# Attention followed by a squared-relu MLP on one core: exp sums ahead of relus, MLP blocks of 192 and 256 tokens, exp sums wholly on VectorE, three transposes one unit later

## Chip, core and metric

The kernel runs on one core of one Trainium2 chip. The metric is the device time of one execution in microseconds (us). Most executions of one kernel agree within 0.3%. A ratio in this document is the mean time of one kernel's fast runs over the mean of the other's fast runs of the same rounds, so it is not quite the ratio of the medians that are quoted beside it. The profiled span is 1.7 to 1.9 us shorter than the time, as it starts with the first instruction and ends with the last.

## The reference, cut to what matters

```python
# q, k, v: 8 batches x 12 heads x 448 tokens x 64; w_in: 768 x 2048; w_out: 2048 x 768
scores = scale * q @ k.T
e = exp(scores - m)
attn = e / (sum(e) + exp(-m) + 1e-9)      # a softmax with one more term in the sum
x = attn @ v                              # rearranged to 3584 tokens x 768
h = x @ w_in
out = relu(h)**2 @ w_out
```

## The kernel before

TensorE does the matmuls, ScalarE (ACT) the exp, VectorE (DVE) the additions, relus and squares. A **unit** is a pair of heads of one batch. Batch 0 is cut in two halves of 192 and 256 tokens, so units 0 to 11 are batch 0, and units 12 to 17 batch 1. The other six batches run in a loop of 18 **cycles** of two units each, three cycles to a batch. MLP work is woven in between: `ins` is a list of tiles of the first matmul (768 to 2048) of the batch before, `outs` one of the second. `drain` takes single matmul pairs from `ins` up to a time, `run` whole tiles, `rows(n)` takes `n` pairs from `outs`.

The MLP tile, with its eviction on VectorE, and the row sums, whose reciprocal takes a Ln and an Exp on ScalarE:

```python
def tile_in(t0, n, f0, per):
    hp = mp_tile()                       # one PSUM bank, one of four in turn
    for j in range(per):                 # per groups of 128 d_ff columns in one bank
        for dc in range(DCH):            # 6 chunks of d_model
            product(...)                 # two matmuls on the two column halves, n columns
    # relu: VectorE, but the tile with t0 == 0 and f0 == 8 on ScalarE
    nc.vector.tensor_mul(gs[...], r, r)

def row_sums(us, sums):
    zp = mp_tile()
    # ... matmuls with ones: the sums over keys (L243)
    nc.scalar.activation(out=rcp, in_=zp, func=AF.Ln, bias=one_b)      # L246
    nc.scalar.activation(out=rcp, in_=rcp, func=AF.Exp, scale=-1.0)    # L247
```

The exp sums of a unit are three VectorE additions of its four key chunks (`add_chunks`, steps 0, 1 and 2, the last adds the two halves). One loop cycle, cut:

```python
scores(ua, ea, 0); rows(11); scores(ua, ea, 1); add_chunks(ua, ..., 0); rows(11)
scores(ub, eb, 0); add_chunks(ua, ..., 1); add_chunks(ua, ..., 2); rows(10)
scores(ub, eb, 1); add_chunks(ub, ..., 0)
# ... values and normalise of the two units of the cycle before
n = (3, 7, 6)[pr // 2]                   # MLP tiles of this cycle
run(ins, n - 3)
add_chunks(ub, eb, sb, hb, 1)
add_chunks(ub, eb, sb, hb, 2)
run(ins, 2)
for at in (i, i + 1):
    rcps[at] = row_sums([units[at]], (ess.pop(at)[0:1],))
run(ins, 1)
```

In the traces VectorE runs its instructions in the order of the program: in the cycle at 117 us three relus start at 112.88, 114.02 and 115.15 us, then the two sums at 116.12 and 116.77, then the fourth relu at 117.31, as the code above has them. So a sum that stands behind a relu in VectorE's queue waits for the MLP tile of that relu, and a relu behind a sum waits for the exps.

The softmax here doesn't subtract the row's maximum and nothing guards it: scores larger than these inputs give would overflow.

## Time and profile before

| | before |
|---|---|
| time, median of three | 427.88 us |
| profiled span | 426.0 us |
| units 12 to 17, apart | 5.3 us |
| loop cycles of a batch (3, 7, 6 tiles) | 15.38, 17.31, 16.18 us |

### The profile page before, as it was taken

To read this page: it belongs to the slowest core of one execution; us is meant where nothing else is said; L and a number is where in the kernel's file an instruction comes from. 1 tells how busy PE (TensorE), PEld (TensorE's weight loads), DVE (VectorE), ACT (ScalarE), POOL (GpSimd) and SP (SyncE) were. 2 spreads that over 40 slices of the span, in tenths; PEclk is the share of its full clock that TensorE was granted. 3 is DMA by queue.
4 is the path that set the end of the run, shared out by engine and by line. 5 is a ranking of instruction groups with operands and counts; after the bars stand their busy time and mean duration, and the time that the engine had idled before them with its cause. 6 is when DMAs were issued, how large, how long until landed. Compare 5 with 4: busy or idle time off the path is not lost.

```text
span 426.0 us, 10689 instructions
## 1 busy us (share of the span) xinstructions
PE 410.8 (96%) x4715; PEld 271.7 (64%) x4715; DVE 278.1 (65%) x537; ACT 236.5 (56%) x328; POOL 36.5 (9%) x58
## 2 busy tenths in 40 slices
PE   8879999899999999999999999999999999999996
PEld 3566666565676675775776765775766766655563
DVE  4766778767775868668675769658676678377000
ACT  3989888664485384583575564773755754200211
POOL 7423310020000200002000300001000000000000
PEclk9999999999999999999999999999999999999999
DMA  9999999789109940199507871098001101100222
GB/s 201 197 198 196 191 199 197 141 124 201 39 2 218 177 110 2 48 183 180 134 2 167 157 143 38 38 194 144 38 2 38 38 2 38 39 37 0 75 74 75
DMA packets 75679, 45.58 MB, mean 107 GB/s; under 512 B 42544, under 2 KB 71856, under 8 KB 75312
## 3 DMA queue, kind: packets, MB, share of 16 engines
q0 software_dynamic: 28848, 22.16, 34.2%
q1 hardware_dynamic: 46064, 22.05, 22.0%
q8 instruction: 37, 0.61, 0.6%
q10 hardware_dynamic: 720, 0.69, 0.5%
q14 instruction: 10, 0.08, 0.1%
HBM read 45.69 MB, written 17.93 MB: 149 GB/s over the span
## 4 chain that ended last, share of the span: by engine, by line
PE 75%; DVE 10%; ACT 6%; DMA 5%; issue 2%; POOL 1%; ACTq 0%; POOLq 0%
PE mp L279 18%; PE mp L329 15%; PE mp L281 11%; PE xp L279 6%; PE sp L194 5%; PE mp L229 5%; PE xp L329 5%; DVE rt L299 4%; DMA kn<-in_k_dram 4%; ACT et L162 3%; PE xp L281 3%; PE xp L229 3%; PE sp L182 3%; DVE es L209 2%; DMA vn<-in_v_dram 2%; DVE half L207 2%
## 5 line engine op out<-in xcount | busy, mean ns | idle before, releaser
L162 ACT ACTIVATE et<-sp 112x896 f16<-112x896 f32 (+2 forms) x192 | 165.2, 913 | 25.8 <-PE sp L182 14.6
L279 PE MATMUL mp<-xt,win 128*64 128x448 f16 (+2 forms) x1260 | 113.2, 324 | 4.1 <-DVE xt L258 1.9
L279 PEld LDWEIGHTS <-win 128*64 128x64 f16 x1536 | 84.8, 110 | 50.4 <-issue 9.1
L329 PE MATMUL mp<-wout,gs 64*128 64x384 f16 x864 | 103.1, 322 | 0.0
L329 PEld LDWEIGHTS <-gs 64*128 64x128 f16 x1152 | 70.8, 94 | 18.5
L299 DVE TENSOR_SCALAR rt<-mp 128x448 f16<-128x448 f32 (+2 forms) x104 | 62.8, 604 | 23.2 <-PE mp L279 19.7
L246 ACT ACTIVATE rcp<-mp,one_b 128x448 f32<-128x448 f32 (+2 forms) x38 | 23.9, 630 | 67.5 <-PE mp L243 67.5
L301 DVE TENSOR_TENSOR gs<-rt 128x448 f16<-128x448 f16 (+2 forms) x132 | 50.8, 385 | 4.9 <-ACT rt L297 0.4
L329 PE MATMUL xp<-wout,gs 64*128 64x384 f16 x288 | 52.6, 322 | 0.0
L207 DVE TENSOR_TENSOR es<-et 112x896 f16<-112x896 f16 x42 | 26.0, 620 | 22.8 <-ACT et L162 22.8
L194 PE MATMUL sp<-qk 64*112 64x224 f16 x480 | 36.7, 261 | 1.2 <-ACT et L162 1.2
L194 PEld LDWEIGHTS <-qk 64*112 64x112 f16 x480 | 29.5, 128 | 9.2 <-issue 7.3
L338 ACT ACTIVATE ot<-mp 128x384 f32<-128x384 f32 x29 | 14.3, 493 | 35.0 <-PE mp L281 26.6
L281 PEld LDWEIGHTS <-gs 128*128 128x128 f16 x240 | 23.4, 98 | 15.8 <-issue 0.4
L229 PEld LDWEIGHTS <-vn 112*64 112x64 f16 x432 | 22.7, 109 | 15.2 <-issue 4.6
L281 PE MATMUL mp<-wout,gs 128*128 128x384 f16 x192 | 31.9, 326 | 0.0
L279 PE MATMUL xp<-xt,win 128*64 128x448 f16 x276 | 30.0, 353 | 0.5 <-DVE rt L299 0.5
L247 ACT ACTIVATE rcp<-rcp 128x448 f32<-128x448 f32 (+2 forms) x48 | 27.7, 577 | 1.5
L340 DVE SCALAR_TENSOR_TENSOR ot<-mp,ot 128x384 f32<-128x384 f32 x27 | 15.1, 558 | 19.4 <-ACT ot L338 18.1
L207 DVE TENSOR_TENSOR half<-et 112x896 f16<-112x896 f16 x42 | 25.9, 617 | 0.0
L299 DVE TENSOR_SCALAR rt<-xp 128x448 f16<-128x448 f32 x27 | 16.8, 623 | 13.0 <-PE xp L281 8.3
L182 PE MATMUL sp<-qk 64*112 64x448 f16 (+2 forms) x192 | 24.0, 321 | 1.2 <-ACT et L162 0.5
(62 smaller groups left out, 316.6 us busy)
## 6 DMA issues: line engine op xcount, KB each, us to landing
vn<-in_v_dram POOLq DMA_DIRECT2D x7, 672.0 KB, 8.5
out_dram<-ot SPq DMA_DIRECT2D x9, 384.0 KB, 2.3
win<-in_moe_w_in_dram POOLq DMA_DIRECT2D x8, 384.0 KB, 14.0
wout<-in_moe_w_out_dram POOLq DMA_DIRECT2D x4, 768.0 KB, 13.6
stage_q<-in_q_dram POOLq DMA_DIRECT2D x4, 676.0 KB, 11.2
stage_k<-in_k_dram POOLq DMA_DIRECT2D x4, 676.0 KB, 14.7
out_dram<-ot SPq DMA_DIRECT2D x8, 288.0 KB, 2.6
out_dram<-ot SPq DMA_DIRECT2D x10, 192.0 KB, 2.7
```

The lines of the kernel that those rows point to most:

```text
L162: nc.scalar.activation(out=out_, in_=in_, func=AF.Exp, scale=scale)
L182: nc.tensor.matmul(sp[:, h, o:o + n], qk[r, 1, x + P * kk:x + P * kk + P], qk[r, 0, x + q0:x + q0 + n], start=True, stop=True)
L194: nc.tensor.matmul(sp[:, odd, h * (S // 2):(h + 1) * (S // 2)], qk[r, which, kx:kx + 2 * P - 1:2], qk[r, 0, x:x + S // 2], start=True, sto ...
L207: nc.vector.tensor_add((es, half[:, 0:2 * S])[step], e[:, 2 * step], e[:, 2 * step + 1])
L229: nc.tensor.matmul(xp[64 * h:64 * h + 64, o:o + n], vns[b][:, 2 * pr + h, kk, :], of_head(chunk(et, u, kk // 2, kk), u, h), start=(kk == 0 ...
L246: nc.scalar.activation(out=rcp[:, 0:m], in_=zp[:, 0:m], func=AF.Ln, bias=one_b)
L247: nc.scalar.activation(out=rcp[:, 0:m], in_=rcp[:, 0:m], func=AF.Exp, scale=-1.0)
L279: nc.tensor.matmul(out_[x:x + 64], lhsT[:, x:x + 64], rhs, start=start, stop=stop)
L281: nc.tensor.matmul(out_, lhsT, rhs, start=start, stop=stop)
L299: nc.vector.tensor_scalar(out=rt[:, 0:m], in0=hp[:, 0:m], scalar1=0.0, scalar2=None, op0=ALU.max)
L301: nc.vector.tensor_mul(gs[:, f0:f0 + per, t0 % RING:t0 % RING + n], r, r)
L329: nc.tensor.matmul(o[:, 0:w], g[x:x + 64], wout[x:x + 64, fb, n0:n0 + w], start=(fb == 0), stop=(fb == NFFB - 1))
```

## The change

It has four parts: in 12 of 18 cycles the second pair's sums stand ahead of all but one relu; batch 0's MLP blocks have 192 and 256 tokens, two d_ff groups to a bank; units 12 to 16 add their exp sums wholly on VectorE (a third addition), so TensorE does one pair of row-sum matmuls instead of two; the transposes of batch 1's first three pairs come one unit later (units 9, 10 and 11; the others were at 12 to 14 already), and so do the first loads of batch 2. The intent is fewer waits of TensorE for VectorE, fewer and wider evictions, and no wait for batch 1's loads.

```diff
-        if t0 == 0 and f0 == 8:
-            nc.scalar.activation(out=rt[:, 0:m], in_=hp[:, 0:m], func=AF.Relu)
-        else:
-            nc.vector.tensor_scalar(out=rt[:, 0:m], in0=hp[:, 0:m], ..., op0=ALU.max)
+        nc.vector.tensor_scalar(out=rt[:, 0:m], in0=hp[:, 0:m], ..., op0=ALU.max)
 ...
-        per = max(1, 512 // n) if n < 256 else 1
+        per = max(1, 512 // n)
 ...
-        transpose_at[NPAIR + 2 + pr + pr // 3] = (1, pr)
+        transpose_at[NPAIR + 3 + pr] = (1, pr)
 ...
-            queue(0, 128)
-            share[0] = left() / NPAIR
+            queue(0, FIRST)                      # FIRST = 192
+            share[0] = left() / (NPAIR + 2)
 ...
-        if i == NPAIR + 4:                       # issues loads of batch 2
+        if i == NPAIR + 5:
 ...
-        drain(share[0] * 0.45)
+        drain(left() * 0.5 if first else share[0] * 0.45)
 ...
-            rcp = row_sums(done, (ess.pop(i - 1),))
+            rcp = row_sums(done, (ess.pop(i - 1)[0:1],))
 ...
-        for step in range(2):
+        for step in range(3):
             add_chunks(u, et, es, half, step)
-            drain(share[0] * 0.2)
+            drain(share[0] * (0.15, 0.1, 0.15)[step])
 ...
-            queue(128, S - 128)
+            queue(FIRST, S - FIRST)
 ...
-        run(ins, n - 3)
+        if pr:
+            run(ins)
+            n -= 1
         add_chunks(ub, eb, sb, hb, 1)
         add_chunks(ub, eb, sb, hb, 2)
-        run(ins, 2)
+        run(ins, n - 1)
         for at in (i, i + 1):
             rcps[at] = row_sums([units[at]], (ess.pop(at)[0:1],))
-        run(ins, 1)
+        run(ins)
```

More of the change, by code (lines that the diff above doesn't have):

```diff
@@ L295, in tile_in @@
         rt = r_pool.tile([128, 512], FP16, name="rt")
-        if t0 == 0 and f0 == 8:
-            nc.scalar.activation(out=rt[:, 0:m], in_=hp[:, 0:m], func=AF.Relu)
-        else:
-            nc.vector.tensor_scalar(out=rt[:, 0:m], in0=hp[:, 0:m], scalar1=0.0, scalar2=None, op0=ALU.max)
+        nc.vector.tensor_scalar(out=rt[:, 0:m], in0=hp[:, 0:m], scalar1=0.0, scalar2=None, op0=ALU.max)
         r = rt[:, 0:m].rearrange("p (j n) -> p j n", j=per)
@@ L514 @@
             done = [prev]
-            rcp = row_sums(done, (ess.pop(i - 1),))
+            rcp = row_sums(done, (ess.pop(i - 1)[0:1],))
             values(prev, ets.pop(i - 1), xp)
         drain(share[0] * 0.15)
-        for step in range(2):
+        for step in range(3):
             add_chunks(u, et, es, half, step)
-            drain(share[0] * 0.2)
-        if i == 3 * NPAIR - 1:
-            add_chunks(u, et, es, half, 2)
-            ess[i] = (es,)
-            if ins and ins[0][0] < ins[0][1]:
-                run(ins)
+            drain(share[0] * (0.15, 0.1, 0.15)[step])
+        if i == 3 * NPAIR - 1 and ins and ins[0][0] < ins[0][1]:
+            run(ins)
         normalise(done, xp, rcp)
         if first:
-            queue(128, S - 128)
+            queue(FIRST, S - FIRST)
             share[0] = left() / (NPAIR + 0.3)
@@ L564 @@
             if at not in rcps:
-                rcps[at] = row_sums([units[at]], (ess.pop(at),))
+                rcps[at] = row_sums([units[at]], (ess.pop(at)[0:1],))
             xp = mp_tile()
@@ L583 @@
         n = (3, 7, 6)[pr // 2]
-        run(ins, n - 3)
+        if pr:
+            run(ins)
+            n -= 1
         add_chunks(ub, eb, sb, hb, 1)
         add_chunks(ub, eb, sb, hb, 2)
-        run(ins, 2)
+        run(ins, n - 1)
         for at in (i, i + 1):
             rcps[at] = row_sums([units[at]], (ess.pop(at)[0:1],))
-        run(ins, 1)
+        run(ins)
         if pr == NPAIR - 2:
```

## The prediction

> **What bounds the kernel now.** I read the page first: the busy line, then the chain that ended last.
>
> ```profile
> PE 410.8 (96%) x4715; PEld 271.7 (64%) x4715; DVE 278.1 (65%) x537; ACT 236.5 (56%) x328; POOL 36.5 (9%) x58
> PE 75%; DVE 10%; ACT 6%; DMA 5%; issue 2%; POOL 1%; ACTq 0%; POOLq 0%
> ```
>
> TensorE has work in flight for 411 of 426 us, so there is little idle time to recover; but a tenth of the chain is DVE. The timeline splits the run in three: 0 to 69.7 us is attention of batches 0 and 1 with the first MLP blocks mixed in (18 units; unit 7 starts near 21.7), 69.7 to 363.7 is a loop of 18 cycles (6 batches of three), and after that TensorE streams matmuls to the end. The change leaves the last part alone. Next I read the waits in total:
>
> ```profile
> PEld L243 <- DVE es L209: 4.5, 13, 0.8
> PE mp L279 <- DVE rt L299: 1.5, 10, 0.2
> PE sp L194 <- ACT et L162: 1.2, 5, 0.3
> ```
>
> In a loop cycle the row-sum matmuls (L243) wait for the exp sums (L209), and the MLP tile behind them waits for a relu (L299) to free its PSUM bank. That is the target of the reordering. The third line is as important: five cycles wait for ScalarE instead. Here is the cycle around 117 us, which has the DVE wait, and then the one around 132 us, a first cycle of a batch, where the sums are already ahead of all relus (timelines; start, duration, engine, line):
>
> ```profile
> 117.21 0.36 PE L243 MATMUL mp<-es,ones 112*64 112x448 f16 x2
> 117.61 0.64 ACT L246 ACTIVATE rcp<-mp,one_b 128x448 f32<-128x448 f32 x1 [5.85 <-PE mp L243]
> 117.98 1.33 PE L279 MATMUL mp<-xt,win 128*64 128x448 f16 x12 [0.15 <-DVE rt L299]
> 119.89 1.71 ACT L162 ACTIVATE et<-sp 112x896 f16<-112x896 f32 x2
> 121.46 0.59 PE L194 MATMUL sp<-qk 64*112 64x224 f16 x8
> 123.63 0.59 PE L194 MATMUL sp<-qk 64*112 64x224 f16 x8
> ```
>
> ```profile
> 132.59 0.36 PE L243 MATMUL mp<-es,ones 112*64 112x448 f16 x2
> 132.97 1.30 PE L279 MATMUL mp<-xt,win 128*64 128x448 f16 x12
> 132.99 0.64 ACT L246 ACTIVATE rcp<-mp,one_b 128x448 f32<-128x448 f32 x1 [1.97 <-PE mp L243]
> 137.03 0.40 PE L194 MATMUL sp<-qk 64*112 64x224 f16 x4 [0.25 <-ACT et L162]
> 139.00 0.60 PE L194 MATMUL sp<-qk 64*112 64x224 f16 x8
> ```
>
> From the first row sum to the second pair's scores the first takes 123.63 - 117.21 = 6.42 us, the second 139.00 - 132.59 = 6.41 us. In the first, the MLP tile starts 0.77 us after the row sum; in the second 0.38 us. The second lost its 0.39 us lead at 137.03, waiting for an exp.
>
> In the first part the timeline shows these stalls:
>
> ```profile
> 26.98 0.39 PE L153 MATMUL mp<-ident,kn 112*64 112x112 f16 x8 [0.99 <-DMA kn<-in_k_dram]
> 28.21 1.02 ACT L162 ACTIVATE et<-sp 112x1024 f16<-112x1024 f32 x1 [1.68 <-PE sp L182]
> 39.06 0.39 PE L153 MATMUL mp<-ident,qn 112*64 112x112 f16 x8
> 44.68 0.60 PE L279 MATMUL mp<-xt,win 128*64 128x320 f16 x6 [0.99 <-DVE xt L258]
> 66.00:71.00 5.00, 5.00 (x62) 3.30 (x58) 4.09 (x10) 4.25 (x7) 0.00 (x0) 1.00 1.28 240
> ```
>
> Batch 1's first transpose waits for its k load; ScalarE idles 1.68 us behind it. At 44.68 an MLP tile of the second block waits for normalised activations. In the last row (a 5 us window; busy PE, PEld, DVE, ACT) TensorE has no gap, and DVE and ScalarE are over 80% busy.
>
> **What the Trainium skill says.** "TensorE: Matmul & The Clock Gate", section "Back-to-back issue gap", says that the spacing of weight-load and matmul pairs is set by both operations, so narrow matmuls cost more than their columns. The trace agrees: at 28.67 us 18 loads and their 128-wide matmuls take 0.60 us, 67 ns a pair on the two column halves, where 128/2.4 is 53; 22 matmuls of 320 columns take 1.50 us of the chain at 52.37, 136 ns a pair, where the columns alone are 133. "VectorE: DVE Perf Modes", section "The TRN2 errata — SBUF-src ops pay a fixed extra latency per instruction", gives a cost of a constant plus elements. The trace agrees in form: relus of 512 and 320 columns take 685 and 486 ns, so 1.04 ns a column and 154 ns fixed. "TensorEngine Tiling (Array Packing)", section "PSUM Bottleneck", advises evacuating several tiles of one bank together, which is what two d_ff groups to a bank do. "Perfetto Trace Analysis", section "Optimization Strategy", says the most contended engine may differ by regime; the windows above agree.
>
> **The change part by part.**
>
> *Sums ahead of relus, 12 of 18 cycles* (a batch's first cycle is the same in both). In the cycle of 117 us VectorE now does relu 1 (112.88), both sums, then relus 2 to 4. With the trace's spacings (relu plus multiply 0.97 us, the two sums 1.19) relu 4 ends near 117.60 in place of 117.93, and the second row sum no longer waits for 117.40. The tile can start at about 117.60: 0.35 us earlier; in the seven-tile cycle 0.40. Taken alone, 12 x 0.38 = 4.5 us. But ScalarE cannot start before the row sum at 117.21, which does not move. Its queue (two Ln, two exp for reciprocals, two exps of scores) runs from 117.61 to 121.60 without a gap, and TensorE needs that last exp's PSUM buffer for the second half of the scores at 121.46. It would arrive near 121.08 and wait. The cycle of 132 us shows this end state, only 0.01 us shorter. So I count 0.01 to 0.02 us a cycle: 0.2 us in all.
>
> *Blocks of 192 and 256 in place of 128 and 320.* Both have 96 column pairs a block (16 groups x 6). Before: 96 x 67 ns + 96 x 133 = 19.2 us of TensorE. After: 96 x 80 + 96 x 107 = 17.9 us, 1.3 less. Evictions on VectorE: before 3 x 685 + 4 x 426 + 16 x (486 + 325) = 16.7 us, plus a relu of 0.59 on ScalarE; after, on the fitted line, 8 x (552 + 359) + 8 x (685 + 426) = 16.2. The one on ScalarE joins them.
>
> *Third add in units 12 to 16.* Five adds of 0.62 us more on VectorE (+3.1), five second row-sum pairs of 0.19 us less on TensorE (-0.95).
>
> *Transposes one unit later.* The 1.0 us stall at 26.98 goes, and unit 8's second exp can follow its predecessor at 26.53 in place of 28.21. TensorE would reach unit 12's scores near 37.3 in place of 38.2. There the load of pairs 3 to 5 lands: issued at 23.84, 14.6 us to landing, so 38.4; the transposes now at 39.06 can begin near 38.5. The drain after them is now half of what is left, 16 pairs of 80 ns (1.28 us) where there were 8 narrow ones (0.54). Unit 12's second scores come out at about 40.1, as now: this lead is gone, except that more MLP work is behind.
>
> *Units 13 to 17.* With pairs of the first block left over, unit 13 need not wait at 44.68 for the normalisation; but ScalarE is then the limit (the exps of unit 12, Ln, exp, exps of unit 13), and only about 0.5 us is left of that 1. Each later unit now takes 5.3 us. It loses one row-sum pair (0.19) and does 19 pairs of 107 ns in place of 18 of 133 (0.37): 5.3 - 0.56 = 4.74 with transposes. ScalarE needs 4 exps in 3.45, Ln 0.65 and exp 0.58: 4.67. So ScalarE caps it almost at once, and VectorE's spacings sum to about 4.4. I allow 0.4 us a unit, not 0.56: 4 x 0.4 = 1.6, plus 0.5 for the start, and 0.2 at unit 15, whose exp wait shrinks. Unit 17 pays back 7 pairs, 0.75 us, for finishing the second block, and the first loop cycle then lacks the six pairs at 78.97 (0.8): a wash, with about 0.7 gained since the next tile starts in the slot where the leftover now waits for a bank.
>
> Sum: 0.5 + 1.6 + 0.2 + 0.7 + 0.2 = 3.2, less 0.3 for queueing between three engines over 90% busy: 2.9 us.
>
> **The rivals.** First, the DVE wait in the loop is pure loss and 4.5 us come back too: 420 us. The totals of waits speak for it, the 6.41 against 6.42 us against it. Second, the third add makes VectorE the bound of units 13 to 17: it is strictly in order, so a relu behind a sum waits for the exps, and row sums then wait for L209. The 4.09 busy in 5 us speaks for it, the wider relus against; all the gain there would go: about 426.5. Third, a load takes the place of the stall removed: loads into batch 1 and the second-batch issues, now a unit later. The 38.4 us landing speaks for it at unit 12, and I counted it; for later ones the queue has work from earlier issues until about 52 us, so they should stay hidden. A full reload stall would cost 1 us: 426.
>
> **Range and chances.** 427.88 - 2.9 = 425.0 us. Low: a third of the loop's waits come back too and units shrink by the full 0.56, 422.8. High: VectorE queueing eats most of the first part, 427.0. Two per cent is 8.6 us, more than all removed waits and work (4.5 + 1.3 + 0.95 + 1.0) if a part of it is hidden as argued: faster 0.02, within 0.97, slower 0.01.
>
> **What would show it.** Right: L243's wait for L209 nearly gone, L194's wait for L162 present in 15 or more cycles with about 4 us in total, and loop cycles of the same length to 0.05 us; the first loop scores (69.71 now) near 67.5; a DMA wait in unit 12's transposes; the 0.99 us at 44.68 gone. Wrong: loop cycles shorter by 0.3 us (rival one), L243 waiting for L209 between 45 and 70 us (rival two), or units of 5.3 us as now.

## More of the kernel before

For units 13 to 17, here are two windows of the profile of the kernel before. The columns are the window, its length, then the busy time and number of instructions of TensorE, its weight loads, VectorE, ScalarE and GpSimd, then the granted TensorE clock, the DMA share and GB/s.

```profile
50.00:55.00 5.00, 5.00 (x60) 3.43 (x58) 4.09 (x10) 4.24 (x6) 4.97 (x7) 1.00 1.29 175
60.00:65.00 5.00, 5.00 (x68) 3.44 (x64) 4.10 (x11) 4.24 (x7) 0.00 (x0) 1.00 1.35 202
```

TensorE has no gap, VectorE is at 82% and ScalarE at 85%. Three engines are close to full, so work that is moved from one to another needs room where it arrives.

To compare traces I use **marks**: the start of the first values matmul (L229) in a unit or a cycle. The code up to unit 6 is the same in all kernels here, but the first mark lies anywhere between 10.7 and 12.0 us in the profiles, so a comparison of marks counts from unit 6.

## The result

The changed kernel takes 425.26 us (median of four, 425.04 to 426.18), against 427.89 us before: a ratio of 0.9945, with a 95% interval of 0.9927 to 0.9962. The 2.6 us lie well outside the spread of both, but under 2%. The profiled span went from 426.0 to 423.3 us. The head and the chain of the changed kernel's page:

```profile
PE 408.8 (97%) x4705; PEld 273.3 (65%) x4705; DVE 277.7 (66%) x535; ACT 235.0 (56%) x327; POOL 36.7 (9%) x58
PE 70%; ACT 17%; DVE 9%; issue 3%; ACTq 0%
```

ScalarE's share of the chain has gone from 6% to 17%, and DMA is no longer on it. The waits of the changed kernel within its loop say why (who waited for whom: us in total, times, longest):

```profile
PE sp L194 <- ACT et L162: 3.4, 15, 0.3
PEld L243 <- DVE es L209: 1.0, 1, 1.0
```

The row sums' wait for the exp sums is down from 13 times to one, and the scores wait for an exp 15 times instead of five. This is the cycle that was shown at 117 us in the prediction, now at 115 us (timeline of the changed kernel):

```profile
114.80 0.55 PE L243 MATMUL mp<-es,ones 112*64 112x448 f16 x4
115.20 0.63 ACT L246 ACTIVATE rcp<-mp,one_b 128x448 f32<-128x448 f32 x1 [5.85 <-DVE rt L296]
115.23 1.33 PE L279 MATMUL xp<-xt,win 128*64 128x448 f16 x12
119.24 0.40 PE L194 MATMUL sp<-qk 64*112 64x224 f16 x4 [0.18 <-ACT et L162]
121.22 0.60 PE L194 MATMUL sp<-qk 64*112 64x224 f16 x8
```

The MLP tile starts 0.43 us after the row sum where it was 0.77. But from the row sum to the second pair's scores it is 121.22 - 114.80 = 6.42 us, as before. The lead is handed over at 119.24.

Where the time went, by marks (values of each unit or cycle), in us from unit 6's mark:

| from unit 6 to | before | after | gained in this step |
|---|---|---|---|
| unit 12 | 20.55 | 20.26 | 0.29 |
| unit 13 | 25.93 | 25.35 | 0.29 |
| unit 17 | 47.14 | 45.05 | 1.51 |
| first loop cycle | 56.59 | 54.98 | -0.48 |
| second loop cycle | 71.71 | 69.00 | 1.10 |
| values after the last cycle | 343.26 | 340.19 | 0.36 |

The sum is 3.07 us; 0.30 of it is lost again because this profile's unit 6 lies at 20.50 in place of 20.20. All loop cycles from the second on have the old lengths to 0.01 us: 18.09, 16.18, 15.37, 17.31. What the loop's new order gains is 0.35 us after the last cycle, where no scores follow that could wait for an exp.

In units 13 to 17 the change did its work, and the profile shows what sets the pace now. First three windows of the changed kernel, then single rows of its timeline:

```profile
50.00:55.00 5.00, 4.69 (x60) 3.02 (x57) 3.30 (x7) 4.74 (x8) 4.39 (x6) 1.00 1.38 192
55.00:60.00 5.00, 5.00 (x74) 3.46 (x73) 4.93 (x10) 4.45 (x7) 0.00 (x0) 1.00 1.33 201
60.00:65.00 5.00, 4.95 (x74) 3.46 (x73) 3.73 (x8) 4.74 (x7) 0.00 (x0) 1.00 1.36 204
```

```profile
38.41 0.39 PE L153 MATMUL mp<-ident,qn 112*64 112x112 f16 x8
45.31 0.40 PE L182 MATMUL sp<-qk 64*112 64x448 f16 x2 [0.41 <-ACT et L162]
65.36 0.38 PE L243 MATMUL mp<-es,ones 112*64 112x448 f16 x2 [0.41 <-DVE qk L157]
```

ScalarE is busy for 95% of the first and third window (4.74 of 5 us), and TensorE has gaps there; between them, TensorE has none and VectorE is busy for 4.93 of 5 us. From the mark of unit 13 to that of unit 17 TensorE waits twice: 0.31 us for an exp in unit 15, and 0.41 us in unit 17. So TensorE's own work sets the pace of these units, but for those two places. Unit 12's transposes (38.41) do not wait for a load, as the prediction had them do. In unit 13 the stall of 0.99 us for normalised activations is gone, and waits for exps stand there instead. In unit 17 a row sum waits for a bank that a VectorE copy has to empty.

### The profile page after: what moved, and what is told of

The parts are those of the page before. It is cut to its first block, busy times and chain, and to the rows that moved or that the text cites. A ratio compares the mean times of both kernels' runs of the same rounds, so it can differ in the third digit from the quotient of the medians.

```text
span 423.3 us, 10664 instructions
## 1 busy us (share of the span) xinstructions
PE 408.8 (97%) x4705; PEld 273.3 (65%) x4705; DVE 277.7 (66%) x535; ACT 235.0 (56%) x327; POOL 36.7 (9%) x58
## 4 chain that ended last, share of the span: by engine, by line
PE 70%; ACT 17%; DVE 9%; issue 3%; ACTq 0%
PE mp L279 17%; PE mp L326 12%; PE mp L281 10%; ACT et L162 9%; PE mp L229 5%; ACT rcp L246 5%; PE xp L279 4%; PE sp L194 4%; PE xp L326 4%; PE xp L281 4%; DVE rt L296 3%; PE xp L229 3%; PE sp L182 3%; ACT rcp L247 3%; DVE gs L298 2%
## 5 line engine op out<-in xcount | busy, mean ns | idle before, releaser
L162 ACT ACTIVATE et<-sp 112x896 f16<-112x896 f32 (+2 forms) x192 | 164.1, 914 | 25.8 <-PE sp L182 13.8
L279 PE MATMUL mp<-xt,win 128*64 128x448 f16 (+2 forms) x1248 | 111.5, 324 | 1.4 <-DVE xt L258 0.8
L194 PE MATMUL sp<-qk 64*112 64x224 f16 x480 | 38.4, 261 | 3.4 <-ACT et L162 3.4
L194 PEld LDWEIGHTS <-qk 64*112 64x112 f16 x480 | 29.9, 128 | 12.6 <-issue 10.8
L279 PE MATMUL xp<-xt,win 128*64 128x448 f16 x288 | 31.3, 352 | 0.0
L281 PE MATMUL mp<-wout,gs 128*128 128x384 f16 x176 | 29.4, 326 | 0.0
L209 DVE TENSOR_TENSOR es<-es,half 112x896 f16<-112x896 f16 x42 | 26.3, 625 | 1.4
```

The source lines that it names most:

```text
L162: nc.scalar.activation(out=out_, in_=in_, func=AF.Exp, scale=scale)
L194: nc.tensor.matmul(sp[:, odd, h * (S // 2):(h + 1) * (S // 2)], qk[r, which, kx:kx + 2 * P - 1:2], qk[r, 0, x:x + S // 2], start=True, sto ...
L279: nc.tensor.matmul(out_[x:x + 64], lhsT[:, x:x + 64], rhs, start=start, stop=stop)
L281: nc.tensor.matmul(out_, lhsT, rhs, start=start, stop=stop)
```

## The experiments

Each experiment was timed in four to six runs, with runs of the kernel before beside it on the same chip. On one chip an execution of the kernel before took 432.69 us and on another 431.42, both with a mean granted clock of 0.984; both count as fast by the rule of states, so the ratios of those rounds have wide intervals, and I quote medians there.

**The loop's new order alone.** The edit is the last hunk of the diff, on the kernel before.

> The kernel before with only the loop's order changed (sums ahead of the relus in 12 cycles). Theory (ScalarE takes over the wait): loop cycles stay at 18.09, 16.18, 15.38, 17.31 us as before; only the stretch after the last cycle, where no scores follow, shortens from 9.12 to about 8.77 us; total 0.3 to 0.5 us less than before. Rival (the reordering is worth the DVE waits it removes): 12 x 0.35 = 4 us less, cycles shorter by 0.35.

Measured: 427.32 us against 427.73, a ratio of 0.9988 (0.9975 to 1.0001). Its cycles last 18.08, 16.18, 15.38 and 17.31 us, and the stretch after the last one 8.77 instead of 9.12. L194 waits for L162 15 times, 3.4 us. The rival, 4 us for 12 waits removed, is out.

**All but the loop's new order.** The same hunk undone in the changed kernel.

> The changed kernel with the loop's old order. Theory: it keeps 2.3 us of the 2.7 us gain; loop cycles of the same length as in both, L243 waits for L209 in the loop again. Rival (most of the gain is the loop's): it keeps under 1 us.

Measured: 425.43 us, a ratio of 0.9949 (0.9935 to 0.9962), so some 2.3 us of the gain stay. L243 waits for L209 13 times again, 4.7 us, and the cycles have the same lengths. With 4.7 us of such waits or with 1.0, the cycle is the same.

**Both row sums one tile earlier.** If ScalarE's queue is the limit, an earlier start of it must pay.

```diff
-        run(ins, n - 1)
+        run(ins, n - 2)
         for at in (i, i + 1):
             rcps[at] = row_sums([units[at]], (ess.pop(at)[0:1],))
-        run(ins)
+        run(ins, 2)
```

> The changed kernel with both row sums of a cycle issued one MLP tile earlier (before the last two tiles), possible because the sums are now ready. ScalarE's queue then starts 1.1 us earlier against TensorE. Theory: the waits of L194 for L162 go; cycles shorten by 0.25 to 0.4 us (in the six-tile cycles about 0.2, as a tile may wait for a relu's bank); total 4 to 6 us less than the changed kernel. Rival (TensorE's own switching sets the cycle): no change, 425.3.

Measured: 420.91 us, a ratio of 0.9846 (0.9826 to 0.9865), 4.5 us less than the run of the first part alone beside it. The cycles are 15.96, 14.92 and 16.92 us, and no L194 waits for L162. The profiled execution (423.05 us) was the slowest of its five. In its first cycle the sums come too early for VectorE. Its timeline, and then its windows:

```profile
81.93 0.38 PE L243 MATMUL mp<-es,ones 112*64 112x448 f16 x2 [1.69 <-DVE es L209]
```

```profile
80.00:84.00 4.00, 2.31 (x18) 1.05 (x16) 2.77 (x6) 2.42 (x4) 0.00 (x0) 0.77 1.15 216
84.00:88.00 4.00, 4.00 (x38) 2.13 (x36) 2.03 (x4) 1.37 (x2) 0.00 (x0) 0.80 1.20 154
```

TensorE waits 1.69 us, and then the granted clock falls to 0.77 and 0.80 of full in two 4 us windows. In windows of 2 us it is 1.00 up to 82 us, then 0.55 and 0.60, and 1.00 again from 86 us. That cycle lasts 16.84 us instead of 14.02.

**One reciprocal for two units.** The second pair of a cycle takes the first pair's reciprocals, so that ScalarE has less to do while TensorE does the same matmuls. The outputs passed the comparison, presumably as the sums of different heads differ little; it is still not a valid kernel.

```diff
-        for at in (i, i + 1):
-            rcps[at] = row_sums([units[at]], (ess.pop(at)[0:1],))
+        rcps[i] = row_sums([units[i]], (ess.pop(i)[0:1],))
+        rcps[i + 1] = row_sums([units[i + 1]], (ess.pop(i + 1)[0:1],), rcps[i])   # matmuls only
```

> Wrong on purpose: the changed kernel, in the loop the second pair takes the first pair's reciprocals, so ScalarE has one Ln and one Exp less (1.15 us) in each cycle; TensorE's work is the same. Theory: L194 no longer waits for L162, each cycle shortens by 0.3 to 0.4 us, total about 6 us less than the changed kernel. Rival (TensorE's own work sets the cycle): 425.3 and the same cycles.

Measured: 417.94 us, a ratio of 0.9773 (0.9759 to 0.9786), 7.5 us less than the first part alone. Cycles: 17.62, 15.79, 14.91, 16.86. In the timeline ScalarE now waits for the scores, not the scores for it:

```profile
116.44 1.73 ACT L162 ACTIVATE et<-sp 112x896 f16<-112x896 f32 x2 [0.47 <-PE sp L194]
```

So ScalarE's queue held the cycle, and TensorE's own work allows 15.79 us in place of 16.18. Whether it is the length of that queue or the place where it ends, the next run tells.

**The row sums divided.** This one is right, and takes nothing from ScalarE's total: the first unit's sums are long ready, so its row sum goes one tile ahead, and the second's stays.

```diff
-        run(ins, n - 1)
-        for at in (i, i + 1):
-            rcps[at] = row_sums([units[at]], (ess.pop(at)[0:1],))
+        run(ins, n - 2)
+        rcps[i] = row_sums([units[i]], (ess.pop(i)[0:1],))
+        run(ins)
+        rcps[i + 1] = row_sums([units[i + 1]], (ess.pop(i + 1)[0:1],))
         run(ins)
```

> The changed kernel with the row sums of a cycle's first pair one MLP tile earlier and those of the second pair where they are now (tile, sum, tile, sum, tile). The results are right. Theory: ScalarE's first Ln and Exp run under the tile, so no exp wait is left, as in the run with one reciprocal: cycles of 17.62, 15.79, 14.91, 16.86 us, total 418 us. Rival (the shorter cycle came from ScalarE's smaller total, not from its place): 425.3.

Measured: 418.20 us against 427.64, a ratio of 0.9772 (0.9734 to 0.9810; as the interval takes in 0.98, "unclear" by the 2% rule, though faster beyond doubt), and correct. Cycles of 17.63, 15.79, 14.92, 16.86 us, some at 15.73. **This version beats both kernels**: by 9.4 us the one before, by 6.9 us the changed one, whose median on the same chip is 425.11. Its timeline for the cycle that has been followed:

```profile
113.81 0.36 PE L243 MATMUL mp<-es,ones 112*64 112x448 f16 x2
114.21 0.63 ACT L246 ACTIVATE rcp<-mp,one_b 128x448 f32<-128x448 f32 x1 [4.67 <-PE mp L243]
115.14 0.36 PE L243 MATMUL mp<-es,ones 112*64 112x448 f16 x2
117.07 1.72 ACT L162 ACTIVATE et<-sp 112x896 f16<-112x896 f32 x2 [0.29 <-PE sp L194]
121.01 0.55 PE L194 MATMUL sp<-qk 64*112 64x224 f16 x8
```

The first Ln (114.21) runs under an MLP tile, and at 117.07 ScalarE waits for the scores. ScalarE does as much as in the changed kernel, so it was the place of its queue that held the cycle, and not its length.

**The divided sums with the old order.** Does the new order matter at all, then?

```diff
-        if pr:
-            run(ins)
-            n -= 1
+        run(ins, n - 3)
         add_chunks(ub, eb, sb, hb, 1)
         add_chunks(ub, eb, sb, hb, 2)
-        run(ins, n - 2)
+        run(ins, 1)
         rcps[i] = row_sums(...)          # then as in the divided version
```

> The same move of the first row sum, but with the exp sums in the kernel before's place behind the relus. Theory: in the 12 cycles with that order the relu and sum waits on VectorE hold TensorE as before, so 18.09, 16.18 and 17.31 us stay; only the first cycle of a batch, which has its sums ahead, shortens from 15.38 to about 14.91; total 423 us. So neither the order nor the move alone pays in the 12 cycles, both together do. Rival (the move alone pays): all cycles shorten, 418 us.

Measured: 420.56 us, where I expected 423: 4.9 us less than the first part alone (425.43), twice the 2.4 that was expected. The first cycle of a batch went to 14.92 us as expected, but of the 12 other cycles about half shortened too: in each batch either the seven-tile or the six-tile cycle lost some 0.35 us. The sums' wait for VectorE is there in each, but the wait for the relu only in six (3 on one pool, 3 on the other; 0.5 us each in total). Two such places in its timeline, the first with the wait, the second without:

```profile
114.92 1.32 PE L279 MATMUL xp<-xt,win 128*64 128x448 f16 x12 [0.15 <-DVE rt L296]
162.93 1.30 PE L279 MATMUL mp<-xt,win 128*64 128x448 f16 x12
```

So the last tile gets, by cycle, a bank that is free or one that a late relu still reads. Why the turn of the banks falls out this way was not settled. The four versions together:

| median, us | sums late, as in the change | first sum one tile earlier |
|---|---|---|
| old order | 425.43 | 420.56 |
| new order | 425.26 | 418.20 |

The new order is worth 0.2 us while ScalarE's queue ends late, and 2.4 us when it doesn't.

**Without the third addition.** Units 12 to 16 sum in two halves on TensorE, as before.

> The changed kernel with units 12 to 16 summing in two halves on TensorE again (five VectorE adds of 0.62 us fewer, five pairs of row-sum matmuls of 0.19 us more). Theory (these units are set by TensorE and ScalarE together): about 0.5 to 0.9 us slower than the changed kernel, units 5.0 us apart in place of 4.81. Rival (the third add makes VectorE the bound, as the 0.41 us wait before unit 17's row sum suggests): 0.4 us faster or more.

Measured: 425.41 us, which is 0.3 us above the changed kernel's 425.11 on the same chip. The units are 5.00 us apart as the theory said; counted from unit 6 the mark of unit 17 comes 0.64 us later. The rival, that the addition costs time, is out for this kernel. The gain is small, under what I expected from the marks; 0.3 us is near the spread of the runs.

**The transposes at their old units**, and the first loads of batch 2 too.

> The changed kernel with batch 1's transposes at their old units. Theory: the 1.0 us wait for the k load at 27 us returns; unit 12 starts about 0.6 us later, and part of it is recovered in unit 12, where ScalarE sets the pace: 0.2 to 0.6 us slower. Rivals: 1.0 us slower (the stall counts in full), or no difference.

Measured: 426.15 us, 1.0 us above the changed kernel on the same chip. So the stall counts in full, as the first rival said; my theory that ScalarE would take part of it back is not borne out. The load waits are back (0.9 us before a weight load, 0.7 before a matmul).

**The old blocks.** The blocks of 128 and 320 tokens, their pace, and the relu on ScalarE; the rest as changed.

> The changed kernel with the MLP blocks of 128 and 320 tokens, their pace and the relu on ScalarE as before; third add, later transposes and the loop's new order stay. Theory (the blocks carry most of the first part's gain): units 13 to 17 go back from 4.81 to about 5.1 us (5.3 less the row-sum pair of 0.19), the first loop cycle from 14.0 to 15.1; 1.3 to 2.2 us slower than the changed kernel. Rival (later transposes and third add carry it): under 0.5 us slower.

Measured: 428.72 us, slower than the kernel before (427.64) and 3.6 us above the changed kernel. This is more than I expected. Two things meet in it. First, VectorE becomes the bound. Waits in its timeline, and a window:

```profile
53.01 0.38 PE L243 MATMUL mp<-es,ones 112*64 112x448 f16 x2 [0.58 <-DVE qk L157]
63.90 0.38 PE L243 MATMUL mp<-es,ones 112*64 112x448 f16 x2 [0.58 <-DVE qk L157]
```

```profile
45.00:50.00 5.00, 5.00 (x44) 2.52 (x42) 2.34 (x7) 2.83 (x4) 0.00 (x0) 0.70 1.32 204
60.00:65.00 5.00, 4.42 (x63) 2.98 (x61) 4.86 (x11) 4.04 (x6) 0.00 (x0) 1.00 1.32 203
```

VectorE is busy for 4.86 of 5 us, the row sums wait for a bank that its copy has yet to empty, and units 15 to 17 are 5.1 to 5.8 us apart. Second, in this profile unit 13 stalls 1.54 us for normalised activations up to 44.63 us, and the granted clock, 1.00 before 44 us, is 0.65 and 0.50 in the next two windows of 2 us. Three of the six executions had a mean clock of 0.994, as this one; whether they stalled too, their times don't show. The three with a mean clock of 0.998 or more took 427.96 to 428.24 us.

**The changed kernel again**, on the same chip and in the same rounds.

> The changed kernel once more, as the reference on the same chip and in the same rounds: 425.0 to 425.6 us.

Measured: 425.11 us, a ratio of 0.9933 (0.9898 to 0.9968).

**The old blocks without the third addition.**

> The run with the old blocks, and the third add taken out as well, so the kernel before with only the later transposes and the loop's new order. Theory (with the old blocks' 20 narrow evictions VectorE has no room for the third add; with the new 16 it has): about 1 to 1.5 us faster than the run with old blocks (428.7), so 427.2 to 427.7, the waits of L243 for a copy (1.7 us in three units) gone, units back to 5.3 us. Rival (the old blocks' loss is TensorE's columns alone): as slow as the old blocks or slower, since 0.95 us of row sums come back.

Measured: 426.41 us, 2.3 us below the old blocks with the third addition, more than expected, and the three waits for the copy are gone. The units are 5.3 us apart as before. (The profiled execution, at 430.67 us, ran at a clock of 0.56 between 10 and 20 us, while the five others had a mean clock of 0.999 or more.) This kernel is the one before with later transposes and the new order, and is 1.2 us faster than it. The four together:

| median, us | two additions | three additions |
|---|---|---|
| blocks of 128 and 320 | 426.41 | 428.72 |
| blocks of 192 and 256 | 425.41 | 425.11 |

The third addition costs 2.3 us with the old blocks (some 1.6 if only executions at full clock are taken) and nothing with the new. The first of the four ran on another chip, where the kernel before took 427.63 us (427.64 on this one). VectorE's busy time fits: from the mark of unit 13 to that of unit 17 it is 4.16 us a unit with the old blocks and two additions and 3.50 with the new, so the new blocks free 0.66 us, and the third addition takes 0.62.

**Both sums early, but not in the first cycle.**

> Both row sums one tile earlier in all cycles but the very first, where in the profile of the earlier run TensorE waited 1.7 us for VectorE and its granted clock then fell to 0.77 and 0.80 for two 4 us stretches. Theory: the first cycle goes back from 16.84 to 14.0 us, the others stay at 15.96, 14.92, 16.92; total 418.5 to 419.5, a little above the version with divided sums. Rival (that clock drop is chance): 420.9 as before.

Measured: 419.57 us, a ratio of 0.9803 (0.9776 to 0.9831; "unclear" by the 2% rule), with a first cycle of 14.00 us, the others unchanged, and the clock at 1.00 throughout. It is 1.3 us below the version with both sums early everywhere. The four executions of that version that were not profiled had a mean clock of 0.999 or more and took 420.3 to 421.1 us; so the clock drop was not in them, and most of the 1.3 us is probably the stall itself, though no trace of an execution with the stall and without the drop was kept.

## Why the prediction was right

The forecast was 425.0 us and the measurement 425.26. The range and the path in the loop are the prediction's merit. That it is within 0.3 us is in part luck: unit 6 alone lies anywhere between 20.2 and 21.4 us in the profiles at full clock, and some steps below were wrong and cancelled. By its steps:

- **The loop's order, 0.2 us of a possible 4.5.** Right. The reordering alone gave 0.4 us, of which 0.35 lies behind the last cycle, a place that the prediction did not name. That ScalarE's queue takes over was read from a cycle that already had the end state, and is shown three ways: the waits moved from 13 on VectorE to 15 on ScalarE, one reciprocal less gave 7.5 us, and the first pair's row sum, Ln and Exp moved one tile earlier gave 6.9 us.
- **The start, 0.5 us at unit 13.** Right in size: 0.58 by the marks. Its mechanism was partly wrong. The prediction had TensorE reach unit 12's scores at 37.3 and wait there for a load until 38.5. It reached them at 37.89, and at 38.41 there was nothing to wait for. Part of it is the later start of that profile (0.3 us); for the rest, the chain of the changed kernel runs through VectorE between 29 and 37 us. Undoing the step costs 1.0 us, more than the prediction gave it.
- **TensorE's columns in the blocks, 1.3 us less.** Wrong: a misread line. The 0.60 us at 28.67 that gave 67 ns for a pair of 128 columns are those of the weight loads, and their first spacing, 0.11 us, is that of the values matmuls of 256 columns just ahead. The matmuls themselves in the timeline of the kernel before:

```profile
28.78 0.67 PE L279 MATMUL mp<-xt,win 128*64 128x128 f16 x18
```

The last of the nine pairs is recorded with 0.22 us, so eight spacings take 0.45 us, 56 ns each. By start times the pairs of 128, 192, 256 and 320 columns stand 56, 82, 109 and 136 ns apart (medians in the traces before and after). A block pair of 128 and 320 then takes 96 x (56 + 136) = 18.4 us, and one of 192 and 256 takes 96 x (82 + 109) = 18.3. So the trace does not agree that narrow matmuls cost more here, and the new blocks move TensorE's work and save almost none of it. What they move lies ahead of unit 12: 81 pairs of 82 ns before its mark in place of 93 of 56, 1.4 us more, which the prediction did not count. The kernel with the old blocks and the later transposes reaches that mark 18.79 us after unit 6, the changed kernel 20.26.
- **Units 13 to 17, 0.4 us each and 0.2 at unit 15.** Predicted 1.8, measured 1.51. The units are 4.81 us apart (predicted 4.9): of the 0.56 us of TensorE's work taken away, 0.49 came, and the cap by ScalarE for which the prediction allowed 0.16 is not there but in unit 15. Without the third addition the units take 5.00, so its 0.19 us count in full. Unit 15's exp wait did not shrink; it went from 0.23 to 0.31 us. Unit 17 is at 5.27, where VectorE's copy, behind the sums, holds a bank for 0.41 us. The allowance for queueing of 0.3 us is just this.
- **The block's remainder.** Predicted -0.75 in unit 17 and +0.8 and +0.7 in the first cycle, 0.75 together; measured -0.48 and +1.10, 0.62 together.
- **What would show it.** The waits of L194 came out as stated (15 cycles; 3.4 us where about 4 was said). The first loop scores were given as near 67.5 us and came at 68.4: the gain is there, but more of it than foreseen is booked in the first cycle behind them.
- **The second rival** was set aside for the right reason, the wider relus. VectorE does become the bound when it gets the third addition, in the kernel with the old blocks, and in the changed kernel in unit 17 alone. How much of the gain hangs on it the prediction did not say.
- **By parts**, from the medians: later transposes and new order 1.2 us, new blocks 1.0 (across two chips), third addition 0.3. The new blocks' 1.0 us can't come from TensorE's columns; by the marks of two profiles it is only 0.2, but one of these ran its start at half clock. Where it comes from is not shown.

## What to carry to other kernels

Before an ordering change is credited with the waits that it removes, look for a stretch of the same trace that already lacks them: if it is no shorter, another engine's queue ends at the same time, and the gain lies in starting that queue earlier. Two such changes can be worth more together than the sum of what they are worth alone: here 0.2 and 4.9 us alone, and 7.2 together. When an engine is given more work, ask what makes room on it: here an addition cost nothing beside the wider evictions, and 1.6 to 2.3 us beside the narrower. And when a cost per instruction is read from a short run, take it from the starts in the middle of the run: its first spacing belongs to what went before.

## What the Trainium skill lacked or had wrong

- "TensorE: Matmul & The Clock Gate", section "Why this matters for your kernels", asks for no TensorE gaps over about 3 us to avoid throughput drops. Here a wait of 1.69 us (TensorE had work in flight for 1.77 of the 4 us up to its end) was followed by a granted clock of 0.55 and 0.60 in two windows of 2 us, and one of 1.54 us by 0.65 and 0.50. That the waits caused it is not shown; four executions of the first kernel had a mean clock of 0.999 or more, and waits of 1.0 us in the kernel before had no such effect in its profile.
- The same page, section "Back-to-back issue gap", on which the prediction rests its 67 ns, gives about 81 ns a matmul of 128 columns in a stream of loads and matmuls, and says that columns / 2.4 + 2.5 ns counts too little there. Here, with loads of 64 columns on the two column halves, whose starts lie 3 ns apart, the pairs stood 56 ns apart for 128 columns, 82 for 192, 109 for 256, 136 for 320 and 189 for 448, which is that formula to 1 ns.
- No page tells how a wait is handed from one engine to another. Here some 0.3 us of waiting for VectorE in each of 12 cycles (4.5 us before, 1.0 after) turned into a wait of 0.2 to 0.3 us for ScalarE, with cycles equal to 0.01 us.
- No page speaks of variation in the first loads. In the profiles of these kernels, one with a slow clock at its start among them, the first values matmul came between 10.7 and 12.0 us with the same code ahead of it. The wait for batch 1's load hid this in the kernel before: with first marks of 10.71 and 11.90 us, the kernel before and the one with only the loop reordered had their unit 12 marks at 40.75 and 40.78. Without that wait, first marks of 10.70 and 11.65 us led to unit 11 marks of 36.43 and 37.37.
